# One batch of logits for two blocks, and the second token tile prepared in three parts, in an attention and gated-MLP kernel

## The chip, the cores and the metric

The kernel runs on one core of one Trainium2 chip. The metric is the device time of one execution in microseconds (us), the median of several. Its span in the profile, from the first to the last instruction, is some 1.7 us shorter. Ratios and 95% intervals are for runs of the same rounds; they are not quite the ratio of the medians quoted beside them, nor always that of the means.

## The reference, cut to what matters

```python
# x: 1 x 2048 x 640, bf16; H = 32 heads of 20; W = 8 keys at distances 0, 2, ..., 14
xn = layernorm(x)
q, k, v = split(xn @ wqkv)
logits = einsum(q, k[pos - off]) * scale      # 8 logits a position and head, -1e9 before the start
attn = softmax(logits)
o = einsum(attn, v[pos - off]) @ wo
out = x + o + ((xn @ w_gate) * (xn @ w_up)) @ w_down      # F = 1536
```

## The kernel before

The Python program holds a small scheduler. Tasks are given with a priority and the PSUM banks they need; the scheduler estimates times, puts tasks in order, and emits one fixed instruction stream per engine. Tokens are cut into 16 tiles of 128 (the front) and 4 blocks of 512 (the rest).

The front of tiles 0 and 1: VectorE computes mean and variance when x has landed, normalises, TensorE transposes five chunks of 128 columns, and each chunk group is copied from PSUM and projected.

```python
    def apply():
        if t < N_SPLIT:
            for a, b in ((0, 384), (384, D)):            # normalise in two parts
                o, i = XNS[:, t, a:b], x[:, a:b]
                op("dve", ...tensor_scalar(o, i, mv[:, 0:1], rstd, ...))
    # ... (cut)
        e = "act" if t == 0 else "dve"
        yield Task(e, lambda: part(0, 3, e), ...)        # copy chunks 0 to 2
        yield Task("act", lambda: part(3, NCH, "act"), ...)   # copy chunks 3 and 4
```

The logits of a block are sums over products, done on TensorE in column tiles of 32, four at a time. The sums of the weighted values (`SEL` as weights) use the same tiles; there are four of them late in the kernel, and "the first sums" below are the first of the four.

```python
    op("pe", ...matmul(o, G[:], x, ..., tile_position=(0, 32 * a)))   # logits
    # ... (cut)
    def gu(j):                                           # gate and up matmuls of block j
        # ... waits (cut)
        for m in range(NF):                              # 12 steps, 2 x 5 matmuls of 512 columns each
            h = ht(j, m)
            # ... (cut)
    FAST = [(2, m) for m in range(NF)]   # steps whose up half ScalarE copies to SBUF before VectorE multiplies
    JOIN = ()
```

In a step that is not in `FAST`, VectorE reads the up half straight from its PSUM bank, and the bank comes free when that multiply is done.

Of the kernel before, what the change touches and what calls it, by code (L numbers as in the profile page):

```python
# [355 lines left out]
def build_kernel(nc, A_x, A_wqkv, A_wo, B_x, B_w_gate, B_w_up, B_w_down, out):  # L356
# [103 lines left out]
    def mark(*k):  # L460
        done.add(k)
# [36 lines left out]
       r=[G[:]], w=[G[:]], name="g2", occ=0.3)  # L498
    op("pool", lambda e: e.memset(KT[:, :, 0:PAD], 0.0), w=[KT[:, :, 0:PAD]], name="kpad", occ=0.3)

    def xslot(t):
        return t + 4 if t < 8 else t - 8

# [55 lines left out]
    def front(t):  # L559
# [31 lines left out]

        def apply():
            if t < N_SPLIT:
                for a, b in ((0, 384), (384, D)):
                    o, i = XNS[:, t, a:b], x[:, a:b]
                    op("dve", (lambda o, i: lambda e: e.tensor_scalar(o, i, mv[:, 0:1], rstd, op0=ALU.subtract, op1=ALU.mult))(o, i),  # L596
                       r=[i, ("mv", t), ("rstd", t)], w=[o], name=f"lnap{t}", occ=0.09 + (b - a) * 0.55e-3)
            elif t < N_DVE_A:
                op("dve", lambda e: e.tensor_scalar(xs, x, mv[:, 0:1], rstd, op0=ALU.subtract, op1=ALU.mult),
                   r=[x, ("mv", t), ("rstd", t)], w=[xs], name=f"lnap{t}", occ=0.45)  # L600
            else:
                op("act", lambda e: e.activation(xs, x, ACT.Identity, bias=nmr, scale=rstd),
                   r=[x, ("nmr", t), ("rstd", t)], w=[xs], name=f"lnap{t}", occ=0.75)
            mark("apply", t)
# [22 lines left out]
        if t < N_PE_T:  # L627
            hold = []

            def trans(*bs):  # L630
                tpvs = [PS[:, b, :].bitcast(BF16)[:, 0:NCH * 128].rearrange("p (c f) -> p c f", c=NCH) for b in bs]
                b, tpv = bs[0], tpvs[0]
                for c in range(NCH):
                    i, q = xs[:, c * 128:(c + 1) * 128], tpvs[c // 3 if len(bs) > 1 else 0][:, c, :]
                    op("pe", (lambda q, i: lambda e: e.transpose(q, i, IDENT[:]))(q, i), r=[i, IDENT[:]], w=[q],  # L635
                       name=f"tr{t}_{c}", occ=0.057, lat=0.2)
                hold.extend(zip(bs, tpvs))
                if t == 0:
                    warm(3)

            def part(lo, hi, eng):
                b, tpv = hold[lo // 3]
                a, i = o[:, lo:hi], tpv[:, lo:hi]
                if eng == "dve":
                    X = op("dve", lambda e: e.tensor_copy(a, i), r=[PS[:, b, :]], w=[a], name=f"xntcp{t}_0", occ=0.1 + 0.08 * (hi - lo))  # L645
                else:
                    X = op("act", lambda e: e.activation(a, i, ACT.Copy), r=[PS[:, b, :]], w=[a], name=f"xntcp{t}_1",
                           occ=0.12 + 0.12 * (hi - lo))
                K.free_bank(b, X)

            def copy():
                b, tpv = hold[0]
                if t < N_DVE_C:
                    X = op("dve", lambda e: e.tensor_copy(o, tpv), r=[tpv], w=[o], name=f"xntcp{t}", occ=0.49)
                else:
                    X = op("act", lambda e: e.activation(o, tpv, ACT.Copy), r=[tpv], w=[o], name=f"xntcp{t}", occ=0.75)
                K.free_bank(b, X)

            yield Task("pe", trans, r=[xs], prio=p, banks=2 if t < N_SPLIT else 1)
            if t < N_SPLIT:  # L660
                e = "act" if t == 0 else "dve"
                yield Task(e, lambda: part(0, 3, e), r=[PS[:, hold[0][0], :]], prio=p - 1)
                yield Task("act", lambda: part(3, NCH, "act"), r=[PS[:, hold[1][0], :]], prio=p - 1)
            else:
                yield Task("dve" if t < N_DVE_C else "act", copy, r=[PS[:, hold[0][0], :]], prio=p)
        else:
            def dmat():
                op("sp", lambda e: e.dma_start_transpose(o, xs), r=[xs], w=[o], dma=True, name=f"dtr{t}", nbytes=200e3, occ=1.25, extra=1.3)

            yield Task("sp", dmat, r=[xs], prio=1)  # L670
# [7 lines left out]
    def wcols(which, c, m):  # L678
        if which == 2:
            return WQKV[:, WPOS[2], c, m * 128:(m + 1) * 128]  # L680
        return WQKV[:, WPOS[which], c, m:D:NCH]
# [27 lines left out]
    def proj_group(items, s0, n, prio, keys):  # L709
        hold = []  # L710

        def spread(*bs):
            which = items[0][0]
            if bs:
                p = PS[:, bs[0], :]
                p = bass.AP(p.tensor, p.offset, [p.ap[0], [n, NCH], [1, n]])
                hold.append((bs[0], [(qk_dst(which, 0, NCH, s0, n), p, NCH * n)]))
            b = hold[0][0]
            for c in range(0, 3) if bs else range(3, NCH):
                for m in range(NCH):  # L720
                    o = PS[:, b + m // 4, m % 4 * n:m % 4 * n + n]
                    l, x = wcols(which, c, m), XNT[:, c, s0:s0 + n]
                    op("pe", (lambda o, l, x, c, m: lambda e: e.matmul(o, l, x, start=(c == 0 and m % 4 == 0), stop=(c == NCH - 1 and m >= 3)))(o, l, x, c, m),  # L723
                       r=[l, x], w=[o], name=f"p{which}_{s0}_{m}_{c}", occ=n / 2400 + 0.0024, lat=0.3)

        def go(b):
            parts, outs, col = [], [], 0
            for which, m0, nm in items:
                for k in range(nm):
                    parts.append((PS[:, b, col + k * n:col + (k + 1) * n], which, m0 + k, s0, n))  # L730
                outs.append((qk_dst(which, m0, nm, s0, n), bank_view(b, col, nm, n), nm * n))
                col += nm * n
            mms(parts, b, f"p{items[0][0]}_{s0}")
            hold.append((b, outs))

        def ev():
            b, outs = hold[0]
            X = evac(outs, f"pev{items[0][0]}_{s0}")
            for i in range(2 if wide else 1):
                K.free_bank(b + i, X)  # L740
            for which, m0, nm in items:
                for k in range(nm):
                    for u in range(n // TS):
                        bump("qk", which, (s0 + u * TS) // JB, m0 + k)

        wide = prio < 10
        if wide:
            yield Task("pe", spread, r=[wcols(items[0][0], 2, 0), XNT[:, 2, s0:s0 + n]], prio=prio, banks=2, contig=True)
            yield Task("pe", spread, r=[wcols(items[0][0], NCH - 1, 0), XNT[:, NCH - 1, s0:s0 + n]], prio=prio)
        else:  # L750
            yield Task("pe", go, r=[wcols(items[0][0], NCH - 1, 0), XNT[:, NCH - 1, s0 + n - TS:s0 + n]], prio=prio, banks=1)
        if wide and s0:
            yield have("sd", 2 + items[0][0])
        yield Task("act", ev, r=[o for _, o, _ in hold[0][1]], prio=5)

    def proj_qk():
# [343 lines left out]

    at_bank = []
    pend = []
    more = []
    sv_of = {}
    used = [-3, -2, -1]
# [19 lines left out]
    def unit(u):  # L1125
# [26 lines left out]
        def mul(x, r0, nr):  # L1152
# [9 lines left out]
            else:  # L1162
                a = bass.AP(at.tensor, at.offset, [at.ap[0], [0, 2], [0, 1], [1, JB]])
                rk = [at]
            op("dve", lambda e: e.tensor_tensor(p, vw, a, ALU.mult), r=[vv] + rk, w=[p], name=f"pv{u}_{x}_{r0}",  # L1165
               occ=0.09 + 1.1 * nr)

        def add(x, u=u, sv=sv, slots=slots, ids=ids):
# [27 lines left out]
        else:  # L1196
            for x in range(2):
# [2 lines left out]
                yield mt(x, 0, 2)  # L1200
                K.spawn(adder(x))
        mark("mul", u)
        pend.append(u)
        if u in BATCH:
            K.spawn(sums(tuple(pend)))
# [38 lines left out]
    def on_pool(j, m):  # L1244
        return count.get(("lg",), 0) >= NJ and m < 11 and ucount[0] - count.get(("hp",), 0) < HP_MAX

    def gu(j):
        if j == 0:
            for m in range(NCH):
                for jj in range(NJ):  # L1250
                    yield num(4, "qk", 1, jj, m)
            for jj in range(NJ):
                yield num(NCH, "v", jj)
        elif j == 1:
            for m in range(NCH):
                for jj in range(NJ):
                    yield num(4, "qk", 0, jj, m)
        elif j == 2:
            yield have("atx", 0)
        if j:  # L1260
            yield have("gu", j - 1)
        for m in range(NF):
            h = ht(j, m)
            if j == 1 and m == 6:
                yield num(NJ - 1, "lg")
            if j == 2 and m == 4:
                yield num(NJ, "lg")
            hold = []

            def go(which, b):  # L1270
# [59 lines left out]
            yield Task("pe", lambda b: go(0, b), prio=50, banks=1, keep=GU_KEEP, r=[WG[:]])  # L1330
            K.spawn(after())
            yield Task("pe", lambda b: go(1, b), prio=49, banks=1, keep=GU_KEEP - 1, r=[WU[:]])
        mark("gu", j)

    def xr_loads():
        yield num(8, "dn", 0)
# [85 lines left out]
        yield Task("pe", down, prio=41, banks=1, keep=0 if count.get(("ot", j), 0) >= NCH else DN_KEEP, r=[WD[:], WO[:]])  # L1422
        K.spawn(tail())

    FAST = [(2, m) for m in range(NF)]
    JOIN = ()
    SLIP = 0.3
    N_PE_T = 4
    BN_AFTER = (4,)
# [47 lines left out]
    K.spawn(vx_loads())  # L1477
    K.spawn(late_loads())
    K.spawn(weighted())
    for j in range(NJ):  # L1480
        K.spawn(gu(j))
    K.spawn(xr_loads())
    for j in range(NJ):
        K.spawn(dn(j))
# [35 lines left out]
```

## Time and profile before

| | before |
|---|---|
| time, median of 3 runs | 267.62 us (267.57 to 267.82) |
| span in the profile | 265.9 us |
| TensorE (PE) busy | 261.3 us, 98% |
| VectorE (DVE) busy | 219.5 us, 83% |
| GpSimd (POOL) busy | 143.5 us, 54% |

A busy PE is not proof that it works at its peak. In this trace it nearly does from 8.8 us on: the starts of consecutive matmuls lie as far apart as their columns need. What can be won is the time between starts that columns do not explain, and the prediction goes through it place by place.

### The profile page before, as it was taken

To read this page: it belongs to the slowest core of one execution; us is meant where nothing else is said; L and a number is where in the kernel's file an instruction comes from. 1 tells how busy PE (TensorE), PEld (TensorE's weight loads), DVE (VectorE), ACT (ScalarE), POOL (GpSimd) and SP (SyncE) were. 2 spreads that over 40 slices of the span, in tenths; PEclk is the share of its full clock that TensorE was granted. 3 is DMA by queue.
4 is the path that set the end of the run, shared out by engine and by line. 5 is a ranking of instruction groups with operands and counts; after the bars stand their busy time and mean duration, and the time that the engine had idled before them with its cause. 6 is when DMAs were issued, how large, how long until landed. Compare 5 with 4: busy or idle time off the path is not lost.

```text
span 265.9 us, 4425 instructions
## 1 busy us (share of the span) xinstructions
PE 261.3 (98%) x1764; PEld 152.4 (57%) x1764; DVE 219.5 (83%) x259; ACT 113.1 (43%) x205; POOL 143.5 (54%) x89
## 2 busy tenths in 40 slices
PE   7999999999999999999999999999999999999996
PEld 5996975444444444444444443776477647764775
DVE  4687899999998699898699899999999999933211
ACT  3468987556622212242358564313431443125000
POOL 3000000000554997289934567999999899990000
PEclk9999999999999999999999999999999999999999
DMA  6964689960479993841297427355973590006001
GB/s 212 371 205 82 126 119 385 402 256 2 121 143 193 236 219 74 168 79 43 56 337 149 102 52 168 89 155 153 179 182 87 143 181 19 0 0 101 26 25 52
DMA packets 39685, 37.84 MB, mean 142 GB/s; under 512 B 15824, under 2 KB 37328, under 8 KB 39632
## 3 DMA queue, kind: packets, MB, share of 16 engines
q1 hardware_dynamic: 36688, 31.35, 43.8%
q0 software_dynamic: 2736, 6.16, 13.6%
q8 instruction: 14, 0.23, 0.4%
q10 hardware_dynamic: 240, 0.05, 0.1%
q14 instruction: 7, 0.06, 0.1%
HBM read 25.07 MB, written 7.23 MB: 121 GB/s over the span
## 4 chain that ended last, share of the span: by engine, by line
PE 97%; DVE 1%; DMA 1%; issue 0%; ACT 0%
PE PS L1274 39%; PE PS L1374 28%; PE PS L691 23%; PE PS L987 2%; PE PS L723 2%; PE PS L1220 2%; DMA XST<-in_A_x_dram 1%; PE PS L635 1%; DVE STATS L567 0%; DVE XNT L1283 0%; PE PS L675 0%; DVE XNS L596 0%; DVE XNT L645 0%; DVE FB L1387 0%; ACT SD L577 0%
## 5 line engine op out<-in xcount | busy, mean ns | idle before, releaser
L1170 POOL TENSOR_TENSOR SV<-PV 128x1024 bf16<-128x1024 f32 x40 | 94.1, 2526 | 14.9 <-DVE LOG L1033 4.0
L1165 DVE TENSOR_TENSOR PV<-VX,PS 128x1024 f32<-128x1024 bf16 (+1 forms) x54 | 90.8, 1730 | 1.2 <-POOL SV L1170 1.1
L691 PE MATMUL PS<-XNT,WQKV 128*128 128x512 bf16 (+2 forms) x390 | 60.9, 316 | 0.0
L1274 PE MATMUL PS<-XNT,WU 128*128 128x512 bf16 x240 | 59.7, 379 | 0.0
L1274 PE MATMUL PS<-XNT,WG 128*128 128x512 bf16 x240 | 59.6, 379 | 0.0
L691 PEld LDWEIGHTS PS<-XNT,WQKV 128*128 128x128 bf16 x390 | 37.8, 112 | 22.1 <-ACT LOG L998 0.8
L1274 PEld LDWEIGHTS PS<-XNT,WU 128*128 128x128 bf16 x240 | 23.3, 98 | 28.6 <-issue 0.4
L1274 PEld LDWEIGHTS PS<-XNT,WG 128*128 128x128 bf16 x240 | 23.5, 98 | 27.8
L919 DVE TENSOR_TENSOR PRF<-PS,KT 128x1024 f32<-128x1024 f32 x32 | 37.9, 1218 | 0.3 <-PE PS L691 0.3
L696 ACT ACTIVATE HT<-PS 128x512 bf16<-128x512 f32 x24 | 14.3, 597 | 41.9 <-PE PS L1274 41.9
L945 POOL TENSOR_TENSOR PRF<-PRF,PRF 128x1024 f32<-128x1024 f32 x8 | 18.8, 2356 | 21.8 <-DVE LOG L1047 20.6
L1374 PE MATMUL PS<-WD,HT 128*128 128x320 bf16 x192 | 28.4, 299 | 0.4 <-DVE XNT L1283 0.4
L696 ACT ACTIVATE FB<-PS 128x320 bf16<-128x320 f32 x24 | 10.5, 437 | 40.6 <-PE PS L1374 40.6
L872 DVE TENSOR_TENSOR PRD<-QT,KT 128x2048 bf16<-128x2048 bf16 x24 | 27.3, 1220 | 0.0
L1374 PE MATMUL PS<-WO,OT 128*128 128x320 bf16 (+1 forms) x165 | 26.6, 295 | 0.0
L1006 POOL MEMSET LOG<- 32x6 bf16 (+6 forms) x7 | 0.4, 95 | 44.3 <-ACT LOG L998 44.3
L1374 PEld LDWEIGHTS PS<-WD,HT 128*128 128x128 bf16 x192 | 18.6, 98 | 8.5 <-DVE XNT L1283 1.3
L1283 DVE TENSOR_TENSOR HT<-HT,PS 128x512 bf16<-128x512 bf16 x24 | 16.4, 685 | 8.0 <-PE PS L1274 7.9
L1374 PEld LDWEIGHTS PS<-WO,OT 128*128 128x128 bf16 x165 | 15.9, 98 | 5.9
L963 POOL TENSOR_TENSOR PRD<-PRF,PRF 128x1024 bf16<-128x1024 f32 x8 | 18.7, 2353 | 0.9 <-DVE PRF L919 0.8
L1283 DVE TENSOR_TENSOR XNT<-XNT,PS 128x512 bf16<-128x512 bf16 x12 | 8.2, 684 | 9.4 <-PE PS L1274 9.4
L567 DVE BATCH_NORM_STATS2 STATS<-XST 128x6 f32<-128x320 bf16 x32 | 14.1, 470 | 2.1 <-DMA XST<-in_A_x_dram 2.1
(69 smaller groups left out, 226.9 us busy)
## 6 DMA issues: line engine op xcount, KB each, us to landing
VX<-v_scratch SPq DMA_DIRECT2D x80, 130.0 KB, 3.0
PRF<-PRF POOLq DMA_DIRECT2D x8, 512.0 KB, 5.2
XST<-in_A_x_dram SPq DMA_DIRECT2D x16, 160.0 KB, 5.4
v_scratch<-VST SPq DMA_DIRECT2D x4, 640.0 KB, 5.8
WG<-in_B_w_gate_dram SPq DMA_DIRECT2D x1, 1920.0 KB, 9.2
WU<-in_B_w_up_dram SPq DMA_DIRECT2D x1, 1920.0 KB, 13.2
out_dram<-in_A_x_dram SPq DMA_DIRECT2D x1, 1920.0 KB, 18.5
WD<-in_B_w_down_dram SPq DMA_DIRECT2D x1, 1920.0 KB, 8.5
```

The costliest lines, as they stand in the source:

```text
L567: op("dve", lambda e: e.bn_stats(o, a), r=[a], w=[("st", t, i)], name=f"bn{t}_{i}", occ=0.49)
L691: op("pe", (lambda o, l, x, c, first: lambda e: e.matmul(o, l, x, start=first, stop=(c == NCH - 1)))(o, l, x, c, first), r=[l, x], w=[o], ...
L696: X = op("act", (lambda o, i: lambda e: e.activation(o, i, ACT.Copy))(o, i), r=[i], w=[o], name=name, occ=0.12 + n * 0.9e-3)
L872: op("dve", lambda e: e.tensor_tensor(s[:], qb, kv, ALU.mult), r=[q, rk], w=[s[:]], name=f"prod{j}_{r}_{c}", occ=1.15, lock=True)
L919: X = op("dve", lambda e: e.tensor_tensor(o[:], qb, kv, ALU.mult), r=[q, rk, ("qev", j, c)], w=[o[:]], name=f"prow{j}_{r}_{c}_{q0}", occ=1.17)
L945: yield Task("pool", lambda: op("pool", lambda e: e.tensor_tensor(x, x, y, ALU.add), r=[x, y] + tokens(), w=[x], name=name, occ=2.36, lock ...
L963: yield Task("pool", lambda: op("pool", lambda e: e.tensor_tensor(o, a, y, ALU.add), r=[a, y] + tokens(), w=[o], name=f"qend{j}_{r}_{q0}", ...
L1165: op("dve", lambda e: e.tensor_tensor(p, vw, a, ALU.mult), r=[vv] + rk, w=[p], name=f"pv{u}_{x}_{r0}", occ=0.09 + 1.1 * nr)
L1170: X = op("pool", lambda e: e.tensor_tensor(o, p[:, :, 0, :], p[:, :, 1, :], ALU.add), r=[p[:]] + tokens(), w=[o], name=f"pva{u}_{x}", occ= ...
L1274: op("pe", (lambda l, x, c: lambda e: e.matmul(PS[:, b, :], l, x, start=(c == 0), stop=(c == NCH - 1)))(l, x, c), r=[l, x], w=[PS[:, b, :] ...
L1283: X = op("dve", lambda e: e.tensor_tensor(h, h, PS[:, hold[1], :], ALU.mult), r=[h, PS[:, hold[1], :]], w=[h], name=f"h{m}_{j}", occ=0.65)
L1374: op("pe", (lambda l, x, i: lambda e: e.matmul(dst, l, x, start=(i == 0), stop=(i == n - 1)))(l, x, i), r=[l, x], w=[PS[:, b, :]], name=f" ...
```

## The change

Its intent: one entry into the small column tiles less (blocks 2 and 3 share a batch of logits), and an earlier start of tile 1's projection. The rest makes the joint batch possible: a new order of gate/up steps to feed TensorE until the later batch, and the two PSUM banks of the attention weights given back after their last use.

```diff
+    PARTS = (((0, 3), (3, NCH)), ((0, 1), (1, 3), (3, NCH)))
+    COPY = (("act", "act"), ("act", "act", "dve"))
-                for a, b in ((0, 384), (384, D)):
+                for a, b in [(128 * lo, 128 * hi) for lo, hi in PARTS[t]]:
 ... (transposes, copies and projection take the parts from PARTS; cut)
-        if wide and s0:
-            yield have("sd", 2 + items[0][0])
+        if wide:
+            yield have("sd", 2 + items[0][0]) if s0 else have("xnt", 1)
 ...
+        if u == NU - 1:
+            for b in at_bank:
+                K.free_bank(b, last[0])
 ...
-    def gu(j):
+    SEQ = [(0, range(NF)), (1, range(6)), (2, (0, 1, 2, 3, 8, 9, 10, 11)), (1, range(6, NF)), (2, range(4, 8)), (3, range(NF))]
+    def gu():
 ... (same steps, in the order of SEQ; cut)
-    FAST = [(2, m) for m in range(NF)]
-    JOIN = ()
+    FAST = [(1, m) for m in range(6, NF)] + [(2, m) for m in range(4, 8)]
+    JOIN = (2, 3)
```

More of the change, by code (lines that the diff above doesn't have):

```diff
@@ L499, in build_kernel, with part_of @@
     op("pool", lambda e: e.memset(KT[:, :, 0:PAD], 0.0), w=[KT[:, :, 0:PAD]], name="kpad", occ=0.3)
+    PARTS = (((0, 3), (3, NCH)), ((0, 1), (1, 3), (3, NCH)))
+    COPY = (("act", "act"), ("act", "act", "dve"))
+    def part_of(t, c):
+        return next(k for k, (lo, hi) in enumerate(PARTS[t]) if lo <= c < hi)
     def xslot(t):
@@ L633, in trans @@
                 for c in range(NCH):
-                    i, q = xs[:, c * 128:(c + 1) * 128], tpvs[c // 3 if len(bs) > 1 else 0][:, c, :]
+                    i, q = xs[:, c * 128:(c + 1) * 128], tpvs[part_of(t, c) if len(bs) > 1 else 0][:, c, :]
                     op("pe", (lambda q, i: lambda e: e.transpose(q, i, IDENT[:]))(q, i), r=[i, IDENT[:]], w=[q],
@@ L639, in trans, with part @@
                     warm(3)
-            def part(lo, hi, eng):
-                b, tpv = hold[lo // 3]
+            def part(k, eng):
+                b, tpv = hold[k]
+                lo, hi = PARTS[t][k]
                 a, i = o[:, lo:hi], tpv[:, lo:hi]
@@ L657, in copy @@
                 K.free_bank(b, X)
-            yield Task("pe", trans, r=[xs], prio=p, banks=2 if t < N_SPLIT else 1)
+            yield Task("pe", trans, r=[xs], prio=p, banks=len(PARTS[t]) if t < N_SPLIT else 1)
             if t < N_SPLIT:
-                e = "act" if t == 0 else "dve"
-                yield Task(e, lambda: part(0, 3, e), r=[PS[:, hold[0][0], :]], prio=p - 1)
-                yield Task("act", lambda: part(3, NCH, "act"), r=[PS[:, hold[1][0], :]], prio=p - 1)
+                for k, e in enumerate(COPY[t]):
+                    yield Task(e, (lambda k, e: lambda: part(k, e))(k, e), r=[PS[:, hold[k][0], :]], prio=p - 1)
             else:
@@ L710, in proj_group, with spread @@
         hold = []
-        def spread(*bs):
+        def spread(k, *bs):
             which = items[0][0]
@@ L718, in spread @@
             b = hold[0][0]
-            for c in range(0, 3) if bs else range(3, NCH):
+            for c in range(*PARTS[s0 // TS][k]):
                 for m in range(NCH):
@@ L747, in proj_group @@
         if wide:
-            yield Task("pe", spread, r=[wcols(items[0][0], 2, 0), XNT[:, 2, s0:s0 + n]], prio=prio, banks=2, contig=True)
-            yield Task("pe", spread, r=[wcols(items[0][0], NCH - 1, 0), XNT[:, NCH - 1, s0:s0 + n]], prio=prio)
+            for k, (lo, hi) in enumerate(PARTS[s0 // TS]):
+                yield Task("pe", (lambda k: lambda *bs: spread(k, *bs))(k), r=[wcols(items[0][0], hi - 1, 0), XNT[:, hi - 1, s0:s0 + n]],
+                           prio=prio, banks=0 if k else 2, contig=not k)
         else:
             yield Task("pe", go, r=[wcols(items[0][0], NCH - 1, 0), XNT[:, NCH - 1, s0 + n - TS:s0 + n]], prio=prio, banks=1)
-        if wide and s0:
-            yield have("sd", 2 + items[0][0])
+        if wide:
+            yield have("sd", 2 + items[0][0]) if s0 else have("xnt", 1)
         yield Task("act", ev, r=[o for _, o, _ in hold[0][1]], prio=5)
@@ L1102, in build_kernel @@
     pend = []
+    last = [None]
     more = []
@@ L1164, in mul @@
                 rk = [at]
-            op("dve", lambda e: e.tensor_tensor(p, vw, a, ALU.mult), r=[vv] + rk, w=[p], name=f"pv{u}_{x}_{r0}",
+            last[0] = op("dve", lambda e: e.tensor_tensor(p, vw, a, ALU.mult), r=[vv] + rk, w=[p], name=f"pv{u}_{x}_{r0}",
                occ=0.09 + 1.1 * nr)
@@ L1245, in on_pool @@
         return count.get(("lg",), 0) >= NJ and m < 11 and ucount[0] - count.get(("hp",), 0) < HP_MAX
-    def gu(j):
-        if j == 0:
-            for m in range(NCH):
-                for jj in range(NJ):
-                    yield num(4, "qk", 1, jj, m)
-            for jj in range(NJ):
-                yield num(NCH, "v", jj)
-        elif j == 1:
-            for m in range(NCH):
-                for jj in range(NJ):
-                    yield num(4, "qk", 0, jj, m)
-        elif j == 2:
-            yield have("atx", 0)
-        if j:
-            yield have("gu", j - 1)
-        for m in range(NF):
+    SEQ = [(0, range(NF)), (1, range(6)), (2, (0, 1, 2, 3, 8, 9, 10, 11)), (1, range(6, NF)), (2, range(4, 8)), (3, range(NF))]
+    def gu():
+        for m in range(NCH):
+            for jj in range(NJ):
+                yield num(4, "qk", 1, jj, m)
+        for jj in range(NJ):
+            yield num(NCH, "v", jj)
+        for j, m in [(j, m) for j, ms in SEQ for m in ms]:
             h = ht(j, m)
+            if j == 1 and m == 0:
+                for mm in range(NCH):
+                    for jj in range(NJ):
+                        yield num(4, "qk", 0, jj, mm)
             if j == 1 and m == 6:
                 yield num(NJ - 1, "lg")
-            if j == 2 and m == 4:
-                yield num(NJ, "lg")
+            if j == 2:
+                yield have("atx", 0)
+                yield have("vst", 3)
+                if 4 <= m < 8:
+                    yield num(NJ, "lg")
+            if j == 3 and m == 0:
+                yield have("gu", 2)
             hold = []
@@ L1332, in gu @@
             yield Task("pe", lambda b: go(1, b), prio=49, banks=1, keep=GU_KEEP - 1, r=[WU[:]])
-        mark("gu", j)
+            bump("gus", j)
+            if count["gus", j] == NF:
+                mark("gu", j)
     def xr_loads():
@@ L1479, in build_kernel @@
     K.spawn(weighted())
-    for j in range(NJ):
-        K.spawn(gu(j))
+    K.spawn(gu())
     K.spawn(xr_loads())
```

## The prediction

> **What bounds the kernel now.** I read the chain of work that ended last first, then the timeline of the matrix engine in three short windows, then the busy times by stage. The chain says who sets the end:
>
> ```profile
> PE 97%; DVE 1%; DMA 1%; issue 0%; ACT 0%
> ...
> 14.85 30.47 PE PS L691 x240
> ...
> 104.08 25.90 PE PS L1274 x120
> ...
> 164.52 0.82 PE PS L1220 x12
> 165.33 0.05 issue
> 165.39 0.69 DVE XNT L1283
> 166.08 0.04 issue
> 166.12 18.65 PE PS L1374 x136
> ```
>
> The columns are start, length (us) and what. TensorE's matmuls are the chain from 8.8 us to 263.6 us, and they are dense: 120 gate and up matmuls in 25.90 us are 0.2158 us each, the streaming time of 512 columns. One break inside the stream is visible: at 165.4 TensorE waits for a VectorE multiply (0.69 us of chain) that gives back a bank of PSUM. I worked the rest out from the start times of single matmuls: apart from that break, the front, and the eight places where small column tiles are used, no start is more than 25 ns later than the size of the matmul before it explains. So only time that TensorE itself loses can be won: at the front, at the tile changes, at 165.4.
>
> The front, all engines of interest around 8 us (start, length, instruction, idle time before it):
>
> ```profile
> 7.36 0.64 DVE L596 TENSOR_SCALAR XNS<-XST,MV,SD 128x384 bf16<-128x384 bf16 x2
> 8.01 0.44 PE L635 MATMUL PS<-IDENT,XNS 128*128 128x128 bf16 x5
> 8.21 0.70 ACT L696 ACTIVATE QT<-PS 128x640 bf16<-128x640 f32 x1 [1.09 <-PE PS L723]
> 8.38 0.36 DVE L645 COPY XNT<-PS 128x384 bf16<-128x384 bf16 x1 [0.38 <-PE PS L635]
> 8.79 2.99 PE L723 MATMUL PS<-XNT,WQKV 128*128 128x128 bf16 x50 [0.34 <-DVE XNT L645]
> ```
>
> The five transposes of token tile 1 start at 8.01, the copy of the first three chunks by VectorE runs 8.38 to 8.74, and the projection begins at 8.79. The last transpose started at 8.23 and takes a slot of 0.056 us, so TensorE loses 8.79 - 8.29 = 0.50 us here. ScalarE meanwhile empties the query projection of tile 0.
>
> A batch of logits, TensorE's row alone:
>
> ```profile
> 99.57 1.24 PE L1274 MATMUL PS<-XNT,WG 128*128 128x512 bf16 x5
> 100.75 1.05 PE L987 MATMUL PS<-PRD,G 128*32 128x512 bf16 x16
> 101.73 2.35 PE L691 MATMUL PS<-XNT,WQKV 128*128 128x512 bf16 x10
> 103.92 0.38 PE L1274 MATMUL PS<-XNT,WU 128*128 128x512 bf16 x1
> ```
>
> and the larger batch of an earlier block:
>
> ```profile
> 45.25 2.34 PE L987 MATMUL PS<-PRD,G 128*32 128x512 bf16 x40
> 47.52 1.71 PE L691 MATMUL PS<-XNT,WQKV 128*128 128x512 bf16 x7
> ```
>
> What the reader is to see is the distance between starts. 16 logits matmuls take 101.73 - 100.75 = 0.98 us, 40 take 47.52 - 45.25 = 2.27 us. So one more costs (2.27 - 0.98)/24 = 0.054 us, and 0.98 - 16 x 0.054 = 0.12 us is lost on leaving the small tiles. Entering loses 100.75 - 99.57 - 5 x 0.2158 = 0.10 us.
>
> **What the Trainium skill says.** "TensorEngine Tiling (Array Packing)", Key Properties: "Changing tiling mode (not just tile) drains the TensorE". The trace agrees: 0.10 + 0.12 = 0.22 us for one excursion into 128x32 tiles and back, in each of the eight. "ScalarE: Activation LUTs", What ACT_TABLE_LOAD costs, gives 186 ns + 0.833 ns a column for an ACTIVATE with immediate scale and bias. This trace has 378 ns for 256 columns and 490 ns for 384, so 0.875 ns a column, and a copy of 128 columns comes out at about 266 ns (an estimate by the trace's slope; the page's formula gives 293). "PSUM — Partial Sum Buffer", The four PSUM rules, counts eight banks; the break at 165.4 agrees as far as it goes: the kernel holds two banks for the attention weights, the sums take five, and TensorE waits until a multiply has read another.
>
> **The change, part by part.**
>
> *One batch of logits for blocks 2 and 3.* It removes one of four excursions (the one at 100.75), and its 16 matmuls move to the other, at 129.9. Removed from TensorE's stream: 0.22 us. None of it lies beside other work, as TensorE is the chain there. Blocks 2 and 3 share one softmax, which waits for both anyway, so nothing needs the early batch but the buffers that it frees: the four product tiles of block 2 now stay taken until block 3 is done, and the second half of block 1's gate/up (6 of 12 steps) may not start until then. Hence the reordered gate/up: before the joint batch TensorE now has 12 + 6 + 8 = 26 steps to do, where it has done 235/10 = 23.5 by 129.98 in this profile (matmuls of L1274 in the chain up to there, 10 a step). It is fed 2.5 x 2.16 = 5.4 us longer, less the 0.98 us of the batch moved away: 4.4 us of margin.
>
> *Tile 1 in parts of 1, 2 and 2 chunks.* The first chunk is transposed at 8.01 and done at 8.23. ScalarE copies it, as the emptying of tile 0's query projection is now put behind: start about 8.27 (0.04 us after the matmul's end, as the VectorE copy here), 266 ns, end 8.53; TensorE starts 0.055 us later, 8.59. Two more chunks follow on ScalarE from about 8.44 to 8.82; the first five matmuls keep TensorE until 8.59 + 0.09 + 4 x 0.056 = 8.90, so they are in time. The last two chunks come from VectorE (starting at about 8.49, some 0.29 us by the slope between its 358 ns for 384 and 492 ns for 640 columns), in time too. Gain 8.79 - 8.59 = 0.20 us. The third normalising instruction costs VectorE some 0.2 us, in time that it is idle (8.00 to 8.38).
>
> *Fast multiplies.* Ten instead of twelve h multiplies take the 424 ns form; two fall back to 685 ns: +0.52 us of VectorE, +2 x 0.6 us less on ScalarE. Off the chain. *Giving the two attention banks back after the last multiply* makes room at the end, where TensorE shows no wait now: 0.
>
> *The break at 165.4.* Its order is new. It is 0.48 us of real idle time; it may vanish or come back at another of the four sums. I count 0.2 us as the mean gain.
>
> Sum: -0.22 - 0.20 - 0.2 = -0.62 us. I take off 0.1 us for a front gain that a later arrival may eat, and new small waits of the reordered stream: -0.5 us, so 267.62 - 0.5 = 267.1 us.
>
> **The rivals.** (1) *Product buffers run out.* With block 2's four tiles kept, block 3's wide products have three or four free tiles in their second half, and a tile is kept for a product, a sum by DMA (5.2 us) and an add (2.35 us). VectorE would stall, the joint batch come late, and TensorE run dry after the 4.4 us. For it: in this stage VectorE and GpSimd share the work closely.
>
> ```profile
> 60.00:118.00 58.00, 58.00 (x282) 26.79 (x280) 52.78 (x57) 20.29 (x34) 34.37 (x20) 1.00 0.69 141
> 118.00:165.00 47.00, 47.00 (x239) 20.95 (x241) 41.34 (x45) 24.66 (x43) 33.13 (x15) 1.00 0.51 127
> 165.00:240.00 75.00, 74.59 (x538) 48.01 (x527) 69.00 (x48) 24.34 (x50) 73.45 (x33) 1.00 0.47 106
> ```
>
> (Per stretch: its length, then busy PE, PEld, DVE, ACT, POOL.) Against it: the last products end at 118.2 and GpSimd then adds without a pause until 127.7, so the products have some 2 us to spare before even the batch is late. If it holds, 268 to 270 us. (2) *VectorE and GpSimd become the bound.* From 165 to 240 GpSimd is busy 73.45 of 75 us, so a product stage that ends 2 to 3 us later moves all weighted sums. For TensorE to feel it, it must run out of other work; it keeps nine gate/up steps of block 3 (19 us) to put between, and the bank release at the end lets it begin the down projection of block 3. So hidden: it makes 0, in a bad case +1 us. (3) *Only the front counts, or only the batch:* if the new order brings as much bank waiting as it saves, the result is 267.4 to 267.6. (4) *The 165.4 break and others vanish wholly:* 266.6 to 266.7.
>
> **Range and chances.** The three certain-looking terms give 267.0 to 267.2; rival 4 sets the low end, 266.6; rival 3 and a mild case of rival 1 the high end, 267.7. Two per cent is 5.4 us, ten times what TensorE loses anywhere outside its matmuls, so faster by 2% is nearly excluded, and slower needs rival 1 at full size. Chances: faster 0.01, same 0.97, slower 0.02.
>
> **What would show it right or wrong.** Right: seven excursions into small tiles instead of eight, one with 32 matmuls of L987 and again some 0.22 us of loss; the first projection of tile 1 at about 8.6, all that follows 0.2 us earlier to beyond 40 us; TensorE at 97% of the chain. Wrong: idle time of TensorE between 120 and 140 us (rival 1), a sum that waits for GpSimd late in the kernel (rival 2), new waits for PSUM banks near the sums, or a front whose gain is gone at 15 us because a transpose waits for VectorE.

## The result, and the profile after

The changed kernel took 267.62 us (267.50 to 267.72, 4 runs) beside 267.61 us of the kernel before. The ratio is 0.9999 with an interval of 0.9981 to 1.0016. The time lies in the predicted range, but the predicted gain of 0.5 us is not there.

The chain of work by engine, kernel after, from its page:

```profile
PE 93%; DVE 3%; DMA 2%; issue 1%; SPq 0%; ACT 0%; DVEq 0%
```

Then pieces of that chain in order of time (start, length, what):

```profile
136.12 27.10 PE PS L1287 x125
163.22 0.67 DVE XNT L1296
...
169.53 0.69 DVE XNT L1296
170.23 0.05 issue
170.27 18.65 PE PS L1389 x136
```

PE's share fell from 97% to 93%, which looks like a new bound on VectorE. It is not one. The chain follows whatever released the last wait, and at 170.2 that is the VectorE multiply of the wait known from 165.4. This time the walk back stays longer with VectorE before it returns to TensorE. The wait itself tells how much was lost. TensorE's row alone at the first sums, kernel before and then after:

```profile
164.45 1.26 PE L1220 MATMUL PS<-SV,SEL 128*32 128x512 bf16 x20
166.12 0.58 PE L1374 MATMUL PS<-WD,HT 128*128 128x320 bf16 x3 [0.41 <-DVE XNT L1283]
```

```profile
168.53 1.26 PE L1231 MATMUL PS<-SV,SEL 128*32 128x512 bf16 x20
170.27 0.85 PE L1389 MATMUL PS<-WD,HT 128*128 128x320 bf16 x5 [0.48 <-DVE XNT L1296]
```

From the first sums matmul to the first down matmul it is 1.67 us before and 1.74 us after. The wait is still there, and a little longer.

The joint batch, TensorE's row alone, kernel after:

```profile
133.04 1.24 PE L1287 MATMUL PS<-XNT,WU 128*128 128x512 bf16 x5
134.21 1.91 PE L994 MATMUL PS<-PRD,G 128*32 128x512 bf16 x32
136.06 1.25 PE L1287 MATMUL PS<-XNT,WG 128*128 128x512 bf16 x5
```

32 matmuls take 1.85 us from start to start, where the two batches before took 0.98 us each. One excursion is gone, as intended, and TensorE does not wait before the batch.

The front, all engines, kernel after (start, length, engine, line, operation, and idle time before it):

```profile
7.51 0.82 DVE L602 TENSOR_SCALAR XNS<-XST,MV,SD 128x128 bf16<-128x128 bf16 x3
7.89 0.80 PE L641 MATMUL PS<-IDENT,XNS 128*128 128x128 bf16 x5
8.15 0.69 ACT L654 ACTIVATE XNT<-PS 128x128 bf16<-128x128 bf16 x2 [0.87 <-PE PS L641]
8.52 0.69 PE L729 MATMUL PS<-XNT,WQKV 128*128 128x128 bf16 x7
8.72 0.29 DVE L652 COPY XNT<-PS 128x256 bf16<-128x256 bf16 x1 [0.38 <-PE PS L641]
```

The projection of tile 1 begins at 8.52, earlier than the 8.79 of before. But the normalising takes 0.82 us instead of 0.64, and the five transposes 0.80 us instead of 0.44, as they now wait for it piece by piece. A few us later (TensorE's row alone), kernel before and then after:

```profile
11.62 0.44 PE L635 MATMUL PS<-IDENT,XNS 128*128 128x128 bf16 x5
11.90 1.56 PE L723 MATMUL PS<-XNT,WQKV 128*128 128x128 bf16 x25
13.29 1.28 PE L691 MATMUL PS<-XNT,WQKV 128*128 128x128 bf16 x20
14.41 0.44 PE L635 MATMUL PS<-IDENT,XNS 128*128 128x128 bf16 x5
```

```profile
11.73 0.44 PE L641 MATMUL PS<-IDENT,XNS 128*128 128x128 bf16 x5
12.01 1.28 PE L729 MATMUL PS<-XNT,WQKV 128*128 128x128 bf16 x20
13.12 1.28 PE L697 MATMUL PS<-XNT,WQKV 128*128 128x128 bf16 x20
14.41 0.45 PE L641 MATMUL PS<-IDENT,XNS 128*128 128x128 bf16 x5
```

Tile 3's transposes start at 14.41 in both. The earlier start has vanished within six microseconds. (Part of it was the earlier start of the transposes, 7.89 against 8.01, which has to do with when x landed and when TensorE reached its full pace; see below.) In the changed kernel five matmuls of tile 1's key projection stand before tile 2's transposes (11.73 against 11.62) and 20 follow them instead of 25, so TensorE reaches tile 3 early and then waits: from the last matmul's start to the transpose 0.225 us instead of 0.056. VectorE's row, kernel after, shows why:

```profile
12.21 0.49 DVE L661 COPY XNT<-PS 128x640 bf16<-128x640 bf16 x1 [0.59 <-PE PS L641]
12.61 0.48 DVE L573 BATCH_NORM_STATS2 STATS<-XST 128x6 f32<-128x320 bf16 x1
```

In VectorE's fixed order the copy of tile 2 waits for tile 2's transposes, and tile 3's remaining statistics and its normalising (ending at 14.36) stand behind that copy.

From the start of tile 3's transposes to the end of the last matmul it is 249.15 us before and 248.98 us after. So the trace itself has 0.17 us of gain, all behind the front.

### The profile page after: what moved, and what is told of

It is laid out like the page before. It is cut to its first block, busy times and chain, and to the rows that moved or that the text cites. A ratio compares the mean times of both kernels' runs of the same rounds, so it can differ in the third digit from the quotient of the medians.

```text
span 265.8 us, 4420 instructions
## 1 busy us (share of the span) xinstructions
PE 261.4 (98%) x1764; PEld 152.4 (57%) x1764; DVE 220.3 (83%) x260; ACT 111.9 (42%) x204; POOL 143.8 (54%) x89
## 4 chain that ended last, share of the span: by engine, by line
PE 93%; DVE 3%; DMA 2%; issue 1%; SPq 0%; ACT 0%; DVEq 0%
PE PS L1287 37%; PE PS L1389 28%; PE PS L697 23%; PE PS L994 2%; PE PS L729 2%; DMA XST<-in_A_x_dram 2%; PE PS L1231 1%; DVE PV L1173 1%; DVE XNT L1296 1%; PE PS L641 1%; DVE STATS L573 0%; SPq L479 0%; DVE XNS L602 0%; DVE FB L1402 0%; ACT SD L583 0%
## 5 line engine op out<-in xcount | busy, mean ns | idle before, releaser
L1296 DVE TENSOR_TENSOR HT<-HT,PS 128x512 bf16<-128x512 bf16 x18 | 12.3, 685 | 8.2 <-PE PS L1287 8.2
L1402 DVE TENSOR_TENSOR FB<-PS,XR 128x320 bf16<-128x320 f32 (+1 forms) x9 | 4.1, 454 | 15.3 <-PE PS L1389 15.3
```

What stands on the lines that cost most here:

```text
L1296: X = op("dve", lambda e: e.tensor_tensor(h, h, PS[:, hold[1], :], ALU.mult), r=[h, PS[:, hold[1], :]], w=[h], name=f"h{m}_{j}", occ=0.65)
```

## The experiments

Two theories stood after the first look. **Theory A:** the batch saves its excursion, the bank wait after the first sums is as before, and the front gives its gain back by tile 3. **Rival B:** the result is chance, or the gain is eaten elsewhere, as said for each run. Each table value below comes from single start times in the run's one profile. "Landing" is when tile 1 of x is in SBUF, and "rest" is the time from tile 3's transposes to the end of the last matmul.

| kernel | landing | tile 1's transposes | its projection | tile 3's transposes | rest |
|---|---|---|---|---|---|
| before | 5.64 | 8.01 | 8.79 | 14.41 | 249.15 |
| after | 5.80 | 7.89 | 8.52 | 14.41 | 248.98 |
| after_again | 5.79 | 7.88 | 8.51 | 14.40 | 248.98 |
| join_only | 5.77 | 7.92 | 8.72 | 14.33 | 248.96 |
| join_again | 5.72 | 7.87 | 8.67 | 14.28 | 248.97 |
| front_only | 5.71 | 8.00 | 8.59 | 14.37 | 249.16 |
| after_nobreak | 5.55 | 7.64 | 8.27 | 14.16 | 248.44 |
| join_nobreak | 5.49 | 7.80 | 8.58 | 14.20 | 248.43 |
| before_nobreak | 5.73 | 8.14 | 8.93 | 14.54 | 248.67 |
| after_tr2first | 5.56 | 7.66 | 8.28 | 14.09 | 248.95 |
| after_ln2 | 5.96 | 8.11 | 8.71 | 14.49 | 248.98 |
| all_fix | 6.12 | 8.21 | 8.84 | 14.56 | 248.43 |
| all_fix_ln2 | 5.52 | 7.72 | 8.30 | 13.92 | 248.43 |
| all_fix_x1 | 3.55 | 8.16 | 8.75 | 14.36 | 248.43 |

The landing moves from profile to profile, and with it the front. That this is chance is not shown: the two kernels profiled twice repeated it to within 0.05 us (after and after_again, join_only and join_again). A second thing moves, and does not repeat: the moment when TensorE's matmuls reach full pace, 0.056 us for 128 columns instead of 0.107. Its first matmul at full pace starts between 4.0 us (all_fix_ln2) and 7.2 us (all_fix_x1), after a first matmul at 1.27 us in all of them; it is about 6.6 us in the kernel before, and 5.2 and 4.2 us in the two profiles of the changed kernel. Where it came at 6.4 us or later (before, front_only, join_nobreak, before_nobreak, all_fix_x1), tile 1's transposes followed tile 0's projection without a wait. Where it came earlier, they waited for tile 1's normalising: before the first of them in six of nine profiles, by 0.14 to 0.47 us, and between them in all nine. No run sets this moment, so its share in the differences of the front is not shown.

The rest does not move: runs with the same later part agree within 0.03 us. So a gain behind the front is read from the rest to a few hundredths of a us, while the timed runs, with intervals of about 0.13% (0.35 us) on either side, only show the larger ones. All results were correct against the reference.

**join_only: the joint batch with the old front**

```diff
-    PARTS = (((0, 3), (3, NCH)), ((0, 1), (1, 3), (3, NCH)))
-    COPY = (("act", "act"), ("act", "act", "dve"))
+    PARTS = (((0, 3), (3, NCH)), ((0, 3), (3, NCH)))
+    COPY = (("act", "act"), ("dve", "act"))
-        if wide:
-            yield have("sd", 2 + items[0][0]) if s0 else have("xnt", 1)
+        if wide and s0:
+            yield have("sd", 2 + items[0][0])
```

> The changed kernel with the front as it was before (tile 1 in parts of 3 and 2 chunks), so only the joint batch and what goes with it. Theory A (the batch saves its one excursion, the front gives its gain back by 15 us): 0.15 to 0.25 us faster than the kernel before, seven excursions in the trace, tile 3's transposes begin at about 14.4 us with no wait, and the time is that of the changed kernel within 0.1 us. Rival B (the batch gains nothing because its saving is eaten by a longer wait at the first sums, and what little was won came from the front): same as the kernel before within 0.05 us, the wait after the first sums longer than 0.48 us by 0.15 us or more.

Measured: 267.40 us beside 267.56 us (ratio 0.9991, 0.9978 to 1.0005), the means 0.21 us apart. Seven excursions; the rest is 0.19 us shorter than before. Between the starts of the last sums matmul and the first down matmul it is 0.845 us, where the kernel before has 0.792 us. So the batch won 0.19 + 0.05 = 0.24 us and the wait took 0.05 of them. Counted start by start it is the same: one excursion with 32 matmuls loses 0.24 us less than two with 16. The trace bears out A for the batch; B's lost saving is not seen. Tile 3's transposes came without a wait.

**front_only: the kernel before with the new front** (the parts of the diff on `PARTS`, `COPY` and the order of emptying, and nothing else)

> The kernel before with only the new front (tile 1 in parts of 1, 2 and 2 chunks). Theory A: projection of tile 1 starts earlier after the transposes, but five matmuls of the key projection of tile 1 now stand ahead of tile 2's transposes, so tile 3's transposes wait on TensorE 0.1 to 0.2 us and start at about the old 14.4 us; time within 0.1 us of the kernel before. Rival B: no wait at tile 3, everything after is 0.15 to 0.2 us earlier and the time is 0.2 us lower.

Measured: 267.62 us beside 267.56 us (ratio 1.0001, 0.9989 to 1.0014). The projection began 0.59 us after the transposes instead of 0.78 us, so 0.20 us were won there. At tile 3 there was the wait (0.223 us from start to start instead of 0.056), its transposes started at 14.37 us, and the rest was 249.16 us as before. A holds: the gain is made at 8.6 us and gone at 14.4 us.

**after_again and join_again: both kernels once more, on one chip**

> The changed kernel once more, on the same chip as the next three. Theory A (batch 0.24 us won, bank wait 0.05 us longer, front nothing or a small loss): from the start of tile 3's transposes to the last matmul's end 248.98 us as before in this kernel's trace, time 0.0 to 0.2 us under the kernel before. Rival B (the front gains 0.2 us as predicted and the first result was chance): 0.3 us or more under the kernel before.

> The joint batch with the old front once more, beside the changed kernel on one chip. Theory A: 0.05 to 0.25 us faster than the changed kernel. Rival B: 0.15 us or more slower than it, as the new front alone should have given.

Measured: 267.49 us and 267.48 us beside 267.66 us (ratios 0.9997 and 0.9995). The traces repeat to 0.01 us: rest 248.98 and 248.97, tile 3 waited for in the first and not in the second. From landing to tile 3's transposes the old front takes 8.56 us in both runs where tile 1's transposes waited for the normalising (join_only, join_again), and the new front 8.61 us (after, after_again, after_nobreak). So the new front loses 0.05 us in that case. B, that the new front gains 0.2 us, is refuted by the traces; the distance that A expected in the timed runs, 0.05 to 0.25 us, is not resolved (the means are 0.06 us apart).

**after_nobreak: ScalarE empties the bank before the first sums**

```diff
-    FAST = [(1, m) for m in range(6, NF)] + [(2, m) for m in range(4, 8)]
+    FAST = [(1, m) for m in range(6, NF)] + [(2, m) for m in range(4, 8)] + [(3, 4)]
```

TensorE's order of instructions is the same.

> The changed kernel, with the up half of the last gate/up step before the first sums emptied by ScalarE into SBUF (one more fast multiply), so that its PSUM bank does not wait for VectorE. Theory A (the wait after the first sums is for that bank, behind VectorE's weighted products): the distance from the last sums matmul to the first down matmul falls from 0.86 us to 0.31 to 0.35 us, and the time by 0.4 to 0.5 us against the changed kernel. Rival B (the wait is for the sums' own banks or for GpSimd): the distance stays over 0.7 us and the time the same within 0.1 us.

Measured: 266.69 us beside 267.56 us (ratio 0.9968, 0.9956 to 0.9981). All engines around the first sums:

```profile
168.29 1.26 PE L1231 MATMUL PS<-SV,SEL 128*32 128x512 bf16 x20
168.39 0.60 ACT L702 ACTIVATE UF<-PS 128x512 bf16<-128x512 f32 x1 [0.48 <-PE PS L1287]
...
169.48 0.58 PE L1389 MATMUL PS<-WD,HT 128*128 128x320 bf16 x3
```

ScalarE, idle there, empties the bank while the sums still run, and the down matmuls begin 1.19 us after the first sums matmul instead of 1.74 us. The distance from the last sums matmul is 0.311 us, what leaving small tiles costs at the other three sums too. The rest falls by 0.54 us. So the wait was for that bank, behind VectorE's queue of weighted products. The timed gain was forecast against the changed kernel, which was not timed in these rounds; against the kernel before it is 0.84 us between the means (interval about 0.5 to 1.2 us), where the rest has 0.71 us. This profile also had its x early, and the interval does not allow more to be read from it.

**before_nobreak: the same repair in the kernel before** (`FAST = [(2, m) for m in range(NF)] + [(3, 2)]`)

> The kernel before with the bank repair alone (the up half of block 3's third gate/up step, the last ahead of the first sums, emptied by ScalarE). Theory A: the wait after the first sums falls from 0.79 us between starts to 0.31 us, the time by 0.4 to 0.5 us; so the wait was there before the change and worth the same without it. Rival B: the wait reappears at one of the other three sums, as their order moves by one step, and the time stays within 0.15 us.

Measured: 267.31 us beside 267.60 us (ratio 0.9988, 0.9975 to 1.0000), the wait gone, the rest 0.48 us shorter, no new wait at the other sums. The repair is worth as much without the change as the wait was long.

**join_nobreak: joint batch, repair, old front** (the edits of join_only and after_nobreak together)

> Joint batch and bank repair with the old front (parts of 3 and 2 chunks). Theory A: 0.7 to 0.8 us faster than the kernel before, and 0.15 to 0.25 us slower than the run with both repairs and the new front: that distance is what the new front is worth when nothing takes it back. Rival B: no difference between the two beyond 0.05 us; then the new front is worth nothing even so.

Measured: 266.80 us beside 267.60 us (ratio 0.9975, 0.9961 to 0.9988). The rest is 248.43 us, 0.72 us under before: the sum of 0.24 us (batch) and 0.48 us (wait). The other half of A failed: against the run with both repairs and the new front (all_fix, below) it is not slower at all. That is what B said.

**after_tr2first: tile 2's transposes ahead of tile 1's key projection**

```diff
                 hold.extend(zip(bs, tpvs))
+                mark("tr", t)
...
         if wide:
+            if s0 and items[0][0] == 1:
+                yield have("tr", 2)
```

> The changed kernel, but the key projection of tile 1 may not begin before tile 2's transposes. Theory A (the front's gain is given back because tile 2's transposes come five matmuls later and tile 3's chain through VectorE and ScalarE hangs on them): the wait before tile 3's transposes falls from 0.17 us to under 0.05 us, these start 0.1 to 0.25 us before 14.4 us, and the time is 0.1 to 0.2 us lower than the changed kernel's. Rival B (tile 3 hangs on the landing of x): the wait stays, or moves to tile 2's transposes, and the time is the changed kernel's within 0.05 us.

Measured: 267.13 us beside 267.56 us (ratio 0.9985, 0.9973 to 0.9998). The wait before tile 3 is gone (0.055 us from start to start). Tile 3's transposes start at 14.09 us, but its x had landed 0.24 us earlier than in the changed kernel's profile. From landing to tile 3 it is 8.53 us, against 8.61 us in the changed kernel and 8.56 us with the old front. The order was one cause, worth 0.08 us here; not all of the 0.20 us came back. Part of the wait moved, as B had it: tile 2's transposes now waited 0.08 us, behind statistics of tile 2 that began late, at 9.09 us, when its x landed. In all_fix, the same front, tile 2 did not wait, and from landing to tile 3 it is 8.44 us.

**all_fix: tr2first and the bank repair together**

> The changed kernel with both repairs: tile 2's transposes ahead of tile 1's key projection, and the bank before the first sums emptied by ScalarE. Theory A (three separate terms that add: batch 0.22 us, bank wait 0.54 us, front 0.15 to 0.25 us): 0.9 to 1.0 us faster than the kernel before, 266.5 to 266.7 us, no wait at tile 3 and 0.31 us after the first sums. Rival B (the front's share is only the chance of when x lands, not the order): the same as the changed kernel with the bank repair alone, within 0.05 us.

Measured: 266.90 us beside 267.60 us (ratio 0.9974, 0.9962 to 0.9987), on the same chip and in the same rounds as join_nobreak with 266.80 us. So A, 0.9 to 1.0 us, failed: the front with the better order was no faster there than the old one. In this profile x landed late (6.12 us), and two waits show: up to 0.254 us between starts of the transposes, and 0.160 us inside tile 1's projection. Both are for tile 1's normalising, which ends 2.54 us after landing in every profile with three parts (but all_fix_x1), and 2.35 us with two.

**after_ln2: normalise in two parts, transpose and copy in three**

```diff
-                for a, b in [(128 * lo, 128 * hi) for lo, hi in PARTS[t]]:
+                for a, b in ((0, 384), (384, D)):
```

> The changed kernel, with tile 1 still normalised in two instructions of 3 and 2 chunks, but transposed, copied and projected in parts of 1, 2 and 2. Theory A (the third normalising instruction delays the last part by 0.19 us on a path that sets the end, as tile 1's normalising starts when x lands and the transposes wait for it): from the landing of tile 1 to the end of its normalising 2.35 us instead of 2.54 us, no gap over 0.1 us among the five transposes, time 0 to 0.15 us under the changed kernel's. Rival B (the three instructions lie in time that VectorE is idle, as I predicted): no difference in where tile 3's transposes start relative to the landing, and the time is the same.

Measured: 267.46 us beside 267.66 us (ratio 0.9993, 0.9980 to 1.0005). The normalising ends 2.35 us after landing, and the wait inside the projection is gone (0.087 us at most between starts). One gap of 0.134 us among the transposes is left, more than I had expected. Landing to tile 3 is 8.53 us instead of 8.61 us. A holds for the third instruction: it lay on the path.

**all_fix_ln2: the joint batch, the repair, the order and the two-part normalising**

> Joint batch, bank repair, tile 2's transposes first, and normalising in two instructions. Theory A: all terms together, 0.85 to 1.0 us under the kernel before, and from the start of tile 3's transposes to the last matmul's end 248.43 us. Rival B: no better than the joint batch and bank repair with the old front (0.7 us under the kernel before in the last runs).

Measured: 266.95 us (266.42 to 267.12) beside 267.66 us (ratio 0.9973, 0.9959 to 0.9986), the means 0.83 us apart. The front of this kernel, all engines:

```profile
7.23 0.64 DVE L602 TENSOR_SCALAR XNS<-XST,MV,SD 128x384 bf16<-128x384 bf16 x2
7.72 0.50 PE L641 MATMUL PS<-IDENT,XNS 128*128 128x128 bf16 x5
7.97 0.55 ACT L655 ACTIVATE XNT<-PS 128x128 bf16<-128x128 bf16 x2 [0.97 <-PE PS L641]
8.25 0.29 DVE L653 COPY XNT<-PS 128x256 bf16<-128x256 bf16 x1 [0.38 <-PE PS L641]
...
8.30 0.59 PE L730 MATMUL PS<-XNT,WQKV 128*128 128x128 bf16 x7
```

From tile 1's transposes (7.72) to its projection (8.30) it is 0.588 us, and from there to tile 3's transposes (13.92 us) 5.615 us: the value of every kernel with the old front, so nothing is given back. Transposes to tile 3 is 6.20 us against 6.40 us in the kernel before, which is the 0.20 us of the prediction. In the timed runs, just short of A's 0.85 us, that cannot be told from join_nobreak (the means 0.83 us and 0.71 us under before, on different chips and in different rounds).

**all_fix_x1: tile 1 of x loaded ahead of the first weights** (all_fix, and the calls `x_load(1)` and `wqkv_load(0, 0, 3)` swapped)

> Both repairs, and the load of tile 1 of x issued before the first query weights instead of behind them. Theory A (the new front starts tile 1's normalising when x lands, at 5.55 to 5.80 us in the profiles so far, and tile 0's matmuls would be done earlier): x lands about 1 us earlier, the weights 0.4 to 0.6 us later, just in time for tile 0; tile 1's transposes start without a wait right after tile 0's projection and the time is 0 to 0.2 us lower than with both repairs alone. Rival B: the weights come too late for tile 0, whose projection starts later by what the load takes, and the time is 0.1 to 0.4 us higher.

Measured: 266.86 us (266.43 to 267.14) beside 267.60 us (ratio 0.9969, 0.9957 to 0.9982). Tile 1 landed at 3.55 us and its normalising ended at 7.90 us, 0.26 us before TensorE came. The three parts then cost nothing: transposes to tile 3 is again 6.20 us. But the profile is not a clean test of the load order. The weights landed at 6.05 us, 0.7 us later than in the changed kernel; the projection of tile 0 began at 6.42 us, later than in most profiles; and its first seven matmuls ran at 0.107 us each instead of 0.056 us, TensorE not having reached its full pace yet. Whether the swap helps by itself stays open: the time is within 0.15 us of all_fix, inside the noise.

## Why the prediction was right or wrong

The range (266.6 to 267.7) and the class were right, but that is owed to the range's width: it took in 267.62 us, no change at all. The gain of 0.5 us was not there: its sum had three terms, and one held.

- **The batch, 0.22 us: right.** Measured 0.24 us in join_only. The 0.02 us on top were not counted: behind the early batch the second matmul came 0.03 us late, and no such delay follows the joint batch. The drain is paid per excursion, not per matmul, as "TensorEngine Tiling (Array Packing)", Key Properties, lets one expect.
- **"Gain 8.79 - 8.59 = 0.20 us": this step failed.** The local gain was right (0.20 us in front_only, with the projection at 8.59 us as forecast; 0.15 us where the transposes waited for the normalising). That it would reach the end was wrong, for two causes that the prediction did not count. First, the scheduler put five matmuls of tile 1's key projection before tile 2's transposes. From these to tile 3's transposes a chain of a copy, statistics, square root, reciprocal and normalising takes 2.68 us in the changed kernel and in front_only alike, and TensorE waited for it. Second, the sentence "in time that it is idle" about the third normalising instruction was wrong: once tile 0 was quick enough, tile 1's normalising was what TensorE waited for, and the instruction added 0.19 us to it. all_fix_ln2 removes both causes and has the 0.20 us in its trace. In the timed runs they are not resolved.
- **"I count 0.2 us as the mean gain" for the wait after the first sums: this step failed too.** It grew by 0.06 us. The two-sided guess had no mechanism: in the new order, too, a step whose bank hung on VectorE's queue stood last before the first sums. after_nobreak shows the cause, and that 0.54 us were to be had.
- **The 0.1 us taken off for such losses was far too small** a share of the terms at risk: 0.2 us (front) and 0.2 us (wait) were lost whole, and 0.06 us on top. What the trace leaves is 0.24 - 0.06 = 0.18 us behind the front, and 0.05 us lost in it. The timed difference of about 0.0 us in the first result and 0.09 us in after_again agrees with that within its noise.
- **The rivals.** Rival 1 (product buffers run out) came in part, and harmlessly: the last products of block 3 ended at 126.1 us instead of 118.2 us, GpSimd's last addition at 130.7 us instead of 127.7 us, and the batch began at 134.2 us after all 26 steps, 4.3 us later than the second batch before. TensorE had no wait there. Whether full buffers or the new place of VectorE's multiplies moved the products was not tested. Rival 2 came in the harmless form: the last sums moved from 240 to 245 us, with down matmuls of block 3 before them and no wait. Rival 3, a new order that brings as much waiting as it saves, is what happened in the main, though only 0.06 us of the new waiting was at a bank and the rest at the front.

The sign of failure named at the end of the prediction, "a front whose gain is gone at 15 us because a transpose waits for VectorE", is the one that showed.

One reading of a page is to be put right: the count of eight banks stands in "PSUM — Partial Sum Buffer", Specifications (TRN2). No run tests it; the sums' five banks show as five copies out of PSUM by ScalarE in each sum.

## What to carry to other kernels

A gain early in a saturated stream counts only if each later hand-over is also ready earlier, so follow the chain to the next two or three points where the engine could wait, and see whether the edit moves other work in front of one. Cutting a step into more parts helps the consumer but lengthens the producer by a fixed cost per part, which matters as soon as the producer is the one being waited for. A visible half microsecond of waiting for a bank is better removed directly, here by letting an idle engine empty it, than left to the luck of a new order: joint batch and bank repair together took about 0.7 to 0.8 us (0.3%) off the kernel before.

## What the Trainium skill lacked or had wrong

- "TensorEngine Tiling (Array Packing)", Key Properties: says that a change of mode drains TensorE, but not what it costs. Here it is 0.24 us for one entry and exit between 128x128 and 128x32 tiles (rest 249.15 us against 248.96 us, with a wait 0.05 us longer); leaving alone shows as 0.312 us between starts where 0.206 us is the pace of the groups.
- "ScalarE: Activation LUTs", What ACT_TABLE_LOAD costs: 186 ns + 0.833 ns a column gives 293, 399 and 506 ns for 128, 256 and 384 columns; it does not say out of which memory. The runs show 277, 378 and 490 ns for bf16 copies out of PSUM: 0.83 ns a column, as the page has it, and 16 to 21 ns less in all. The slope of 0.875 ns in the prediction came from two sizes alone, and its 266 ns were 11 ns short.
- "VectorE: DVE Perf Modes", The TRN2 errata: "a single large tile pays it once; many small tiles pay it per-tile" agrees with the runs. What one part more costs in a chain of instructions is not there: here 0.19 us for a third part of the same 640 columns, with 315, 341 and 378 ns for normalising 128, 256 and 384 columns.
- "TensorE: Matmul & The Clock Gate", What you observe: the change of pace comes "±500ns run-to-run". Here, over 14 kernels whose matmuls all begin at 1.27 us, the first at full pace lies between 4.0 us (all_fix_ln2) and 7.2 us (all_fix_x1), some 1.6 us to either side of the middle. It is not quite the page's case, as TensorE pauses for 0.1 to 0.8 us before tile 0's transposes. The late change slowed tile 0's projection in all_fix_x1.
- No page that I read says how much a load's landing moves: tile 1 of x, issued at the same place, landed in one profile or another between 5.49 and 6.12 us, which moves the start of the saturated part. That spread is larger than most terms.
